# A sparse-attention and gated-MLP kernel on one core: the first batch in query thirds over all heads, with the gated MLP dealt out matmul by matmul

## The chip, the core and the metric

The kernel runs on one core of a Trainium2 chip. The core has five engines with instruction queues of their own: TensorE (PE in the profile, its weight loads PEld) multiplies matrices into the PSUM memory, VectorE (DVE) and ScalarE (ACT) work elementwise on PSUM and SBUF, GpSimd (POOL) works on SBUF, and SyncE (SP) issues most DMA transfers. Each engine takes its instructions in order. The metric is the device time of one execution in microseconds, lower is better.

## What is computed

Two stages follow each other. The first is block-sparse attention over 4 batches, 8 heads, 768 positions and head size 64. Positions form 24 blocks of 32. A block may attend to itself and its two neighbours, to the first and last block, from the first and last block, and to three sampled blocks. The mask depends on the sampled blocks and is the same for all batches and heads.

```python
scores = scale * np.matmul(q, k.transpose(0, 1, 3, 2))
scores = np.where(mask, scores, -1000000000.0)
attn = np.exp(scores - np.max(scores, axis=-1, keepdims=True))
attn = attn / (np.sum(attn, axis=-1, keepdims=True) + 1e-09)
attn_out = np.matmul(attn, v)
```

The second is a gated MLP (gMLP) per batch, on the heads side by side, x = [768, 512]:

```python
h = np.maximum(x @ w_in, 0.0)                       # 512 -> 1024
u, v = h[..., :512], h[..., 512:]
v_n = (v - mean(v)) / np.sqrt(var(v) + 1e-06)
v_s = np.einsum('ts,bsd->btd', w_spatial, v_n) + b_spatial[None, :, None]
out = (u * v_s) @ w_out
```

Each gMLP batch needs the attention of all eight heads; position t of v_s needs v_n of all 768 positions of that batch.

## The kernel before, in words

Rows 0 to 63 of the tiles `qt` and `kt` hold a head's transposed queries and keys. Rows 64 to 87 hold the mask: on the key side a one-hot row per block (`ind`), on the query side, per key block, 0 or a large negative number (`bm` times `ind`). One product over 88 rows so gives masked scores, and no maximum is subtracted.

**Attention slots.** Work goes in slots. A slot of `qk_exp` (lines 239 to 251) makes one chunk of 128 keys against all 768 queries of a head: two score matmuls of 384 columns (L244) into one of two two-bank PSUM buffers (`sc`), and one exp of 768 columns by ACT (L248) into `a_all`. A head has six slots, a batch 48, the whole kernel 192. Seven slots later (`LAG = 7`) `av` makes one chunk of 128 queries times the values: six matmuls of 65 columns (L260), the 65th column being the sum of the exps. After a head's six, `norm` (L273, L274) divides on DVE, and after a pair of heads `xtr` transposes the result, by DMA from the SP queue (L287), for the last pair of a batch by PE (L283).

**Loads.** Each pair of heads is loaded as fp32 from the SP queue (L95), cast to bf16 by POOL (L109 keys and queries, L112 values) and transposed: pairs 0 to 4 by PE (L191 one head at a time, L199 by pair) with DVE copies out of PSUM (L183, L202), later pairs by two DMA transposes (L227), keys and queries apart, and DVE copies `split_pair` (L233). The weights come by three DMAs on the POOL queue that cast on the way (L439, L446, L449). The spatial weights are transposed by PE and copied by DVE in pairs 2 and 3 (L296, L300).

**gMLP.** `moe_units` makes 24 units per batch: six v units (L332, relu and statistics on DVE, std and power on POOL at L345 and L347), six u units (L355, relu on ACT at L358, normalise on DVE at L359), six spatial units (L377, gate on DVE at L380, gated rows transposed by a DMA each, L384), six output units (L395, copies by ACT and DVE in turn, L400 and L402, store by SP, L403). A unit is four matmuls of 512 columns, a spatial unit six. When a batch's attention is complete, eight slots into the next batch, its units are queued and spread over 48 slots by a budget; a unit's matmuls always stand together. The last batch's gMLP has no attention beside it; it turns through the free PSUM buffers (`moe_ps`), evicts v on ACT (L336), and transposes its gated rows by PE (`g_tr`, L368).

**The order.** The schedule is written out by hand (`manual_schedule`): the loop over pairs and slots at the end of the kernel issues, per slot, the scores, set-up pieces, gMLP units, AV matmuls and transposes in this order, and so sets the order in every engine's queue. Before the first slot eight matmuls on zeros are issued to PE (L145).

Of the kernel before, what the change touches and what calls it, by code (L numbers as in the profile page):

```python
# [10 lines left out]
FP32 = mybir.dt.float32  # L11
# [15 lines left out]
def kernel(  # L27
# [31 lines left out]
    MASK_NEG = -300.0  # L59
    VA = D + 1  # L60
    KR = D + NB

# [9 lines left out]
    ws_nat = const.tile([128, NCH, S], BF16)  # L72
    w_spt = const.tile([128, NCH, S], BF16)
    b_col = const.tile([128, NCH], FP32)
    mhalf = const.tile([128, NCH], FP32)

    qt = [const.tile([KR, S], BF16, name=f"qt{s}") for s in range(4)]
    kt = [const.tile([KR, S], BF16, name=f"kt{s}") for s in range(4)]
    vv = [const.tile([128, 2, NCH, VA], BF16, name=f"vv{s}") for s in range(3)]
# [4 lines left out]
    def dram(src, b, h0, nh):  # L84
        return src[b, h0:h0 + nh].rearrange("h (p c) d -> p h (c d)", c=NCH)

    def st_tile(p, nm):
        st[nm, p] = work.tile([128, 2, NCH * D], FP32, tag=f"st_{nm}", bufs=2, name=f"st_{nm}")
        return st[nm, p]

    def load(p, names="qkv", eng=nc.sync):
        b, g = divmod(p, NG)
        for nm, src in (("q", q), ("k", k), ("v", v)):
            if nm in names:
                eng.dma_start(out=st_tile(p, nm), in_=dram(src, b, 2 * g, 2))  # L95
# [3 lines left out]
    def nat_tile(p, nm):  # L99
        nat[nm, p] = work.tile([128, NCH, 2, D], BF16, tag=f"nat_{nm}", bufs=2,  # L100
                               name=f"nat_{nm}")

    def cast_qk(p, nm, hs, eng):
        src = st[nm, p][:, hs].rearrange("p h (c d) -> p h c d", d=D)
        dst = nat[nm, p].rearrange("p c h d -> p h c d")[:, hs]
        if eng is nc.scalar:
            nc.scalar.activation(out=dst, in_=src, func=AF.Copy)
        else:
            eng.tensor_copy(out=dst, in_=src)  # L109

    def cast_v(p):
        nc.gpsimd.tensor_copy(  # L112
            out=vv[p % 3][:, :, :, 0:D],
            in_=st.pop(("v", p)).rearrange("p h (c d) -> p h c d", d=D))

    def prepare(p):
        for nm in "kq":
            nat_tile(p, nm)
            cast_qk(p, nm, slice(0, 2), nc.gpsimd)
        cast_v(p)  # L120

    samp_i = const.tile([NB, 2 * NR], I32)
    stq, stk = st_tile(0, "q"), st_tile(0, "k")
    nc.scalar.dma_start(out=stk[:, 0:1], in_=dram(k, 0, 0, 1))
    nc.scalar.dma_start(out=stk[:, 1:2], in_=dram(k, 0, 1, 1))
    nc.sync.dma_start(out=samp_i, in_=_listify(sampled_blocks).bitcast(I32))
    for h in range(2):
        nc.sync.dma_start(out=stq[:, h:h + 1], in_=dram(q, 0, h, 1))
    load(0, "v", nc.sync)
    load(1, "qkv", nc.sync)  # L130
    nc.sync.dma_start(out=b_col, in_=moe_b_spatial.rearrange("(p c) -> p c", c=NCH))

    ind_nat = const.tile([NB, S], BF16)
    ind = const.tile([NB, S], BF16)
    allowed = const.tile([NB, NB], FP32)
    tiny = const.tile([128, 1], FP32)
    nc.vector.memset(warm, 0.0)
    nc.vector.memset(allowed, 0.0)
    nc.vector.memset(ind_nat, 0.0)
    nc.vector.memset(tiny, 0.0)  # L140
    nc.scalar.activation(out=tiny, in_=tiny, func=AF.Exp)

    wps = psum.tile([128, 512], FP32, tag="moe", bufs=2)
    for _ in range(8):
        nc.tensor.matmul(out=wps, lhsT=warm[:, 0:128], rhs=warm, start=True, stop=True)  # L145


    colidx = const.tile([NB, NB], FP32)
    nc.gpsimd.iota(colidx, pattern=[[1, NB]], base=0, channel_multiplier=0,
                   allow_small_or_imprecise_dtypes=True)  # L150
    for c in (-1, 0, 1):
        nc.gpsimd.affine_select(out=allowed, in_=allowed, compare_op=ALU.not_equal,
                                fill=1.0, base=c, pattern=[[1, NB]], channel_multiplier=-1)
    for c in (0, NB - 1):
        nc.gpsimd.affine_select(out=allowed, in_=allowed, compare_op=ALU.not_equal,
                                fill=1.0, base=-c, pattern=[[0, NB]], channel_multiplier=1)
    nc.gpsimd.affine_select(out=ind_nat, in_=ind_nat, compare_op=ALU.not_equal, fill=1.0,
                            base=0, pattern=[[-1, NB], [0, BLK]], channel_multiplier=1)
    make_identity(nc, ident)
    nc.gpsimd.tensor_copy(out=ind, in_=ind_nat.rearrange("b (p c) -> b c p", c=NCH))  # L160

    for s in range(3):
        nc.gpsimd.memset(vv[s][:, :, :, D:VA], 1.0)
    nc.gpsimd.memset(mhalf, -0.5)

    nc.vector.memset(allowed[:, 0:1], 1.0)
    nc.vector.memset(allowed[:, NB - 1:NB], 1.0)
    nat_tile(0, "q"), nat_tile(0, "k")
    samp_f = const.tile([NB, 2 * NR], FP32)
    nc.vector.tensor_copy(out=samp_f, in_=samp_i)  # L170
    for r in range(NR):
        nc.vector.scalar_tensor_tensor(out=allowed, in0=colidx,
                                       scalar=samp_f[:, 2 * r:2 * r + 1], in1=allowed,
                                       op0=ALU.is_equal, op1=ALU.max)
    bm = const.tile([NB, NB], BF16)
    nc.vector.tensor_scalar(out=bm, in0=allowed, scalar1=1.0, scalar2=-MASK_NEG,
                            op0=ALU.subtract, op1=ALU.mult)
    cast_qk(0, "q", slice(0, 1), nc.vector)
    cast_qk(0, "k", slice(0, 1), nc.scalar)
    nc.vector.tensor_copy(out=kt[0][D:KR, :], in_=ind)  # L180

# [6 lines left out]
    def tr_head(h, nm, copy):  # L188
        ps = psum.tile([128, S], BF16, tag="moe", bufs=2)
        for c in range(NCH):  # L190
            nc.tensor.transpose(out=ps[0:D, c * 128:(c + 1) * 128], in_=nat[nm, 0][:, c, h],  # L191
                                identity=ident)
        copy((qt if nm == "q" else kt)[h][0:D, :], ps[0:D, :])

    def tr_pair(p, nm):
        src = nat.pop((nm, p))
        ps = psum.tile([128, S], BF16, tag="moe", bufs=2)
        for c in range(NCH):
            nc.tensor.transpose(out=ps[:, c * 128:(c + 1) * 128],  # L199
                                in_=src[:, c].rearrange("p h d -> p (h d)"), identity=ident)  # L200
        for h in range(2):
            nc.vector.tensor_copy(out=(qt if nm == "q" else kt)[(2 * p + h) % 4][0:D, :],  # L202
                                  in_=ps[h * D:(h + 1) * D, :])

    tr_head(0, "k", dve_copy)
    mq = psum.tile([128, 1024], FP32, tag="sc", bufs=2, name="mq")
    for hf in range(2):
        nc.tensor.matmul(out=mq[0:NB, hf * 512:hf * 512 + HALF], lhsT=bm,
                         rhs=ind[:, hf * HALF:(hf + 1) * HALF], start=True, stop=True)
# [43 lines left out]
    def av(j, qc):  # L253
# [10 lines left out]
        if qc == NCH - 1:  # L264
            a_ref.pop(j)
# [240 lines left out]
```

## Time and profile before

| what | value |
|---|---|
| median of 3 runs | 231.86 us (231.13 to 235.44) |
| profiled execution: span, first to last instruction | 228.9 us |
| mean granted TensorE clock | 0.975 |
| PE / PEld busy | 217.0 us (95%) / 130.9 us (57%) |
| ACT busy | 171.3 us (75%), of it exps 144.2 |
| DVE / POOL busy | 131.9 us (58%) / 52.8 us (23%) |
| first exp starts / 12th ends / 48th ends | 7.64 / 20.4 / 47.0 us |
| last batch's gMLP | 199.9 to 225.3 us |
| HBM read / written | 24.38 MB / 6.29 MB |

The profile is one execution; its span lies 2.96 us below the median of the runs, which hold the time around the first and last instruction as well. A busy engine in the row PE need not be a PE at its peak, since matmuls overlap and their ends are modelled: what a matmul costs in a dense row of them is the distance between the starts of two groups. In the rows by stage, the seventh number is the granted clock (1.00 is full speed), then the share of the DMA engines that was busy and the GB/s they moved. An engine that is idle costs nothing unless the chain of work runs through it.

### The profile page before, as it was taken

The page shows a single profiled execution, that of the slowest core. Times are in us where ns is not written, and L with a number is a line of the kernel's source. Part 1 is how long each engine was busy: PE and PEld are TensorE (multiplying, and loading weights), DVE is VectorE, ACT ScalarE, POOL GpSimd, SP SyncE. Part 2 cuts the span into 40 slices and gives each one's busy share as a digit, 9 for nine tenths or more (in the row PEclk, how much of TensorE's full clock was granted, in tenths as well). Part 3 has the DMA queues.
Part 4 walks back from the last instruction along what each step waited for, and adds up shares of the span by engine and source line. Part 5 has one row for each costly group of instructions (what it writes and reads, how often), then busy time and mean ns, then how long its engine had stood idle before and what let it go on. Part 6 is the DMA issues. An engine that isn't in the chain of part 4 may idle for free.

```text
span 228.9 us, 5246 instructions
## 1 busy us (share of the span) xinstructions
PE 217.0 (95%) x2105; PEld 130.9 (57%) x2134; DVE 131.9 (58%) x285; ACT 171.3 (75%) x244; POOL 52.8 (23%) x83
## 2 busy tenths in 40 slices
PE   7799999999999999999999999999999999999993
PEld 3356677766566555665656555566656555544551
DVE  6643545647996545349995344269992423575532
ACT  3668999998799767786799666977798677256341
POOL 7440560421153401210172201210250000012000
PEclk9758999999999999999999999999999999999998
DMA  6589999999418273989838364999050423520015
GB/s 212 201 244 223 356 171 217 271 249 302 149 34 219 86 143 52 275 288 288 243 70 243 64 112 82 265 327 258 3 103 3 80 49 78 198 83 0 0 47 229
DMA packets 54940, 37.31 MB, mean 163 GB/s; under 512 B 38404, under 2 KB 51204, under 8 KB 54788
## 3 DMA queue, kind: packets, MB, share of 16 engines
q1 hardware_dynamic: 53428, 33.83, 54.7%
q0 software_dynamic: 1200, 2.75, 7.1%
q10 hardware_dynamic: 288, 0.39, 0.5%
q8 instruction: 16, 0.26, 0.5%
q14 instruction: 8, 0.07, 0.2%
HBM read 24.38 MB, written 6.29 MB: 134 GB/s over the span
## 4 chain that ended last, share of the span: by engine, by line
PE 76%; ACT 17%; DVE 2%; issue 2%; DMA 1%; ACTq 0%
PE ps L244 22%; ACT a_all L248 17%; PE ps_av L260 11%; PE ps_moe L377 10%; PE ps_moe L332 7%; PE ps_moe L395 7%; PE ps_moe L355 7%; PE ps_t L377 2%; PE ps_t L332 2%; PE ps_t L395 2%; PE ps_t L355 1%; PE ps_sc L377 1%; DMA samp_i<-in_sampled_blocks_dram 1%; PE ps_sc L355 1%; PE ps_sc L395 1%
## 5 line engine op out<-in xcount | busy, mean ns | idle before, releaser
L248 ACT ACTIVATE a_all<-ps 128x768 bf16<-128x768 f32 x192 | 144.2, 810 | 32.6 <-PE ps L244 32.0
L244 PE MATMUL ps<-qt,kt 88*128 88x384 bf16 x384 | 96.0, 332 | 5.2 <-ACT a_all L248 4.1
L260 PEld LDWEIGHTS <-a_all 128*128 128x128 bf16 x1152 | 62.0, 99 | 31.8 <-issue 0.7
L260 PE MATMUL ps_av<-vv,a_all 128*128 128x65 bf16 x1152 | 68.4, 195 | 0.0
L244 PEld LDWEIGHTS <-kt 88*128 88x128 bf16 x384 | 28.4, 99 | 11.0 <-issue 7.4
L380 DVE SCALAR_TENSOR_TENSOR gn<-ps_moe,b_col,un 128x512 bf16<-128x512 f32 x18 | 13.5, 751 | 27.6 <-PE ps_moe L377 27.6
L112 POOL CAST vv<-st_v 128x768 bf16<-128x768 f32 x16 | 13.6, 850 | 52.7 <-PE ps_av L260 43.1
L377 PE MATMUL ps_moe<-vn,w_spt 128*128 128x512 bf16 x99 | 24.8, 378 | 0.5
L377 PEld LDWEIGHTS <-w_spt 128*128 128x128 bf16 x144 | 13.8, 97 | 14.3
L345 POOL TENSOR_SCALAR std<-mv 128x3 f32<-128x3 f32 x8 | 1.9, 243 | 74.0 <-DVE mv L342 61.8
L109 POOL CAST nat_k<-st_k 128x768 bf16<-128x768 f32 x15 | 12.5, 836 | 27.3 <-issue 11.5
L274 DVE TENSOR_TENSOR xn<-ps_av,rc 128x384 bf16<-128x384 f32 x32 | 17.8, 557 | 1.4 <-DVE rc L273 0.3
L332 PE MATMUL ps_moe<-w_in_t,xt 128*128 128x512 bf16 x66 | 18.1, 378 | 0.3
L395 PE MATMUL ps_moe<-w_out_t,gt 128*128 128x512 bf16 x66 | 18.1, 378 | 0.3
L355 PE MATMUL ps_moe<-w_in_t,xt 128*128 128x512 bf16 x66 | 17.7, 378 | 0.3
L341 DVE BATCH_NORM_STATS2 stats<-vsb 128x6 f32<-128x512 bf16 x24 | 16.7, 694 | 1.9 <-ACT vsb L336 1.3
L332 PEld LDWEIGHTS <-xt 128*128 128x128 bf16 x96 | 9.3, 97 | 10.0 <-issue 0.7
L402 DVE COPY osb<-ps_moe 128x512 f32<-128x512 f32 x9 | 6.2, 692 | 15.0 <-PE ps_moe L395 14.9
L355 PEld LDWEIGHTS <-xt 128*128 128x128 bf16 x96 | 9.3, 97 | 9.5
L273 DVE RECIPROCAL rc<-ps_av 128x6 f32<-128x6 f32 x32 | 6.0, 186 | 13.4 <-PE ps_av L260 13.3
L395 PEld LDWEIGHTS <-gt 128*128 128x128 bf16 x96 | 8.9, 97 | 8.4
L359 DVE TENSOR_SCALAR vn<-vsb,mv,rstd 128x512 bf16<-128x512 bf16 x24 | 12.7, 564 | 0.6 <-POOL rstd L347 0.5
(85 smaller groups left out, 181.4 us busy)
## 6 DMA issues: line engine op xcount, KB each, us to landing
st_v<-in_v_dram SPq DMA_DIRECT2D x16, 384.0 KB, 6.2
out_dram<-osb SPq DMA_DIRECT2D x24, 256.0 KB, 2.3
st_q<-in_q_dram SPq DMA_DIRECT2D x15, 384.0 KB, 4.1
st_k<-in_k_dram SPq DMA_DIRECT2D x15, 384.0 KB, 4.7
ws_nat<-in_moe_w_spatial_dram POOLq DMA_DIRECT2D x1, 1152.0 KB, 12.5
w_in_t<-in_moe_w_in_dram POOLq DMA_DIRECT2D x1, 1024.0 KB, 11.8
w_out_t<-in_moe_w_out_dram POOLq DMA_DIRECT2D x1, 512.0 KB, 12.0
st_k<-in_k_dram ACTq DMA_DIRECT2D x2, 192.0 KB, 2.9
```

Source lines behind the costliest of these rows:

```text
L112: nc.gpsimd.tensor_copy(out=vv[p % 3][:, :, :, 0:D], in_=st.pop(("v", p)).rearrange("p h (c d) -> p h c d", d=D))
L244: nc.tensor.matmul(out=ps[:, hf * 512:hf * 512 + HALF], lhsT=kt[j % 4][:, ci * 128:(ci + 1) * 128], rhs=qt[j % 4][:, hf * HALF:(hf + 1) * ...
L248: nc.scalar.activation(out=a_ref[j][:, ci, :].rearrange("p (b c) -> p b c", b=2), in_=ps.rearrange("p (b c) -> p b c", b=2)[:, :, 0:HALF], ...
L260: nc.tensor.matmul(out=av_ref[j][:, qc, :], lhsT=a_ref[j][:, ci, qc * 128:(qc + 1) * 128], rhs=vv[p % 3][:, h, ci, :], start=(ci == 0), st ...
L274: nc.vector.tensor_tensor(out=xn_ref[p][:, :, h, :], in0=ps[:, :, 0:D], in1=rc.to_broadcast([128, NCH, D]), op=ALU.mult)
L332: nc.tensor.matmul(out=ps, lhsT=xt(g)[:, tcc * 128:(tcc + 1) * 128], rhs=w_in_t[:, g, DH:DFF], start=(g == 0), stop=(g == NDM - 1))
L341: nc.vector.bn_stats(out=stats, in_=vsb[:, tcc, :])
L355: nc.tensor.matmul(out=ps, lhsT=xt(g)[:, tcc * 128:(tcc + 1) * 128], rhs=w_in_t[:, g, 0:DH], start=(g == 0), stop=(g == NDM - 1))
L359: nc.vector.tensor_scalar(out=vn[:, tcc, :], in0=vsb[:, tcc, :], scalar1=mv[:, tcc, 0:1], scalar2=rstd[:, tcc:tcc + 1], op0=ALU.subtract, ...
L377: nc.tensor.matmul(out=ps, lhsT=w_spt[:, sc, tcc * 128:(tcc + 1) * 128], rhs=vn[:, sc, :], start=(sc == 0), stop=(sc == NCH - 1))
L380: nc.vector.scalar_tensor_tensor(out=gn[:, tcc, :], in0=ps, scalar=b_col[:, tcc:tcc + 1], in1=un[:, tcc, :], op0=ALU.add, op1=ALU.mult)
L395: nc.tensor.matmul(out=ps, lhsT=gt[:, tcc, dhc, :], rhs=w_out_t[:, dhc, :], start=(dhc == 0), stop=(dhc == NDH - 1))
```

## The change

**First batch in thirds.** Batch 0 is no longer done head after head. Its 36 slots go over three thirds of the queries (256 each), within a third over the four pairs of heads, three slots a pair. A slot makes four score matmuls of 256 columns and one exp of 1024 columns; three slots later `av_third` makes eight AV matmuls; after three of these the pair's third is normalised, and transposed by PE into the unused end of the AV bank (`xtr_third`), with a DVE copy. Batches 1 to 3 keep the slots of before.

```diff
+    NT = 3
+    S0 = NT * NG * 3
+    def qk_third(u, e):
+        t, p = divmod(u, NG)
...
+        ps = psum.tile([128, 1024], FP32, tag="sc", bufs=2)
+        for i in range(4):
+            h, ci = divmod(4 * e + i, NCH)
+            nc.tensor.matmul(out=ps[:, i * TW:(i + 1) * TW],
+                             lhsT=kq[:, 2 * p + h, ci * 128:(ci + 1) * 128],
+                             rhs=kq[:, 2 * p + h, qcols(t)], start=True, stop=True)
+        out = a_ref[u].rearrange("p h c n -> p (h c n)")[:, 4 * e * TW:4 * (e + 1) * TW]
+        nc.scalar.activation(out=out, in_=ps, func=AF.Exp, scale=0.125)
+    def av_third(u, e):
...
+        for i in range(8 * e, 8 * e + 8):
+            g, ci = divmod(i, NCH)
+            h, qc = divmod(g, TC)
+            nc.tensor.matmul(out=av_ref[u][:, qc * 2 + h, :],
+                             lhsT=a_ref[u][:, h, ci, qc * 128:(qc + 1) * 128],
+                             rhs=vv[p % NVV][:, h, ci, :],
+                             start=(ci == 0), stop=(ci == NCH - 1))
+    def xtr_third(u):
+        t, p = divmod(u, NG)
+        xtr_pe(p, xn_ref.pop(u), t * TC, TC, x_ref.pop(u))
```

**Keys and queries in one tile.** `kq` holds keys and queries of eight heads, 88 rows by 2 x 768 columns a head; `vv` has six buffers for three. For batch 0 all keys and the first query third are loaded, cast and transposed first (`tr_first`, a PE group of eight per pair, two DVE copies of 64x1024), then the other two thirds (`tr_rest`). The mask rows are copied to the heads by DVE and, for heads 4 to 7, by one DMA (`block_rows`). The mask is built from iotas and comparisons on DVE, and the sampled blocks are read as integers.

```diff
-    qt = [const.tile([KR, S], BF16, name=f"qt{s}") for s in range(4)]
-    kt = [const.tile([KR, S], BF16, name=f"kt{s}") for s in range(4)]
-    vv = [const.tile([128, 2, NCH, VA], BF16, name=f"vv{s}") for s in range(3)]
+    kq = const.tile([KR, H, 2 * S], BF16, name="kq")
+    NVV = 6
...
+    ts(lim[MR], hot[MR], 1.0 - BLK, ALU.max, BLK - 1.0, ALU.min)
+    tt_op(kq[MR, 0, K_].rearrange("b (c p) -> b c p", c=NCH), hot[MR], lim[MR], ALU.is_equal)
...
+    def second_head():
+        dve_copy(kq[0:D, 1, qcols(0)], psq[D:128, 0:TW])
+        ps = k_head(1)
+        dve_copy(kq[MR, 1, 0:S + TW], kq[MR, 0, 0:S + TW])
+        dve_copy(kq[0:D, 1, K_], ps[0:D, 0:S])
+        filler(2, wps)
...
+    def tr_first(p):
+        src = nat.pop(p)
+        ps = bank()
+        for c in range(NCH + TC):
+            tr(ps, c, pair_of(src, c))
+        for h in range(2):
+            dve_copy(kq[0:D, 2 * p + h, 0:S + TW], ps[h * D:(h + 1) * D, :])
```

The eight matmuls on zeros become six, two before the first scores and two in `second_head`.

**Merged DMA transposes.** From pair 4 on, one DMA transpose takes keys and queries of a pair together, and each head is copied out by one DVE copy of 64x1536 (`split`). Gated rows are transposed two chunks at a time. The spatial weights go by DMA transposes too.

```diff
-        nc.sync.dma_start_transpose(out=tt[nm, p],
-                                    in_=nat.pop((nm, p)).rearrange("p c h d -> p (c h d)"))
+    def tr_dma(p):
+        tt[p] = work.tile([128, 2 * NCH, 128], BF16, tag="tt", bufs=2, name="tt")
+        nc.sync.dma_start_transpose(out=tt[p], in_=nat.pop(p).rearrange("p c h d -> p (c h d)"))
```

**Weights.** The three casting DMAs of the POOL queue are gone. SP loads w_in in eight pieces, w_out in four and w_spatial in six, as fp32, the first two into the four buffers of `osb`; POOL casts them.

**gMLP by single matmuls.** Every product becomes a list of single matmuls, the last of which runs the eviction. `run_queue` takes so many of them per slot that the list lasts for the slots given. Batch 0 is dealt in three parts as its thirds end, batches 1 and 2 over 48 slots each as before. v is normalised in place, the gate is written over u, and the tiles `un`, `vn`, `gt` have one buffer for two. u products stand between v products, with two u products behind the last v (in the last batch three, u3 to u5), where six stood before. The last batch transposes its gated rows by DMA, the last two chunks singly, and its last output product is made in two halves.

```diff
+        when(17, c(moe_begin, 0), lambda: deal(moe[0].in_steps(0, TC, TC), 12))
+        when(29, lambda: deal(moe[0].in_steps(TC, TC, TC), 12))
+        when(41, lambda: deal(moe[0].in_steps(2 * TC, TC, TC) + moe[0].rest_steps(), S0 + 8 + 48 - 41))
...
+    def run_queue():
+        if not queue or pace["slots"] <= 0:
+            return
+        pace["credit"] += (len(queue) - pace["credit"]) / pace["slots"]
+        pace["slots"] -= 1
+        n = int(pace["credit"] + 0.5)
+        for _ in range(min(n, len(queue))):
+            queue.popleft()()
+            pace["credit"] -= 1
...
+            if self.last:
+                seq = [(nm[0], int(nm[1])) for nm in "v0 v1 u0 v2 u1 v3 v4 u2 v5 u3 u4 u5".split()]
```

**Schedule.** The set-up pieces hang on slot numbers (`when`). For a pair p of batches 1 to 3 whose first slot is g, the loads are issued at slot g-34 (not before 14), the casts at g-21, the DMA transpose at g-18, the two `split` copies at g-5 and g-3:

```diff
+    when(0, second_head,
+         c(cast, 1, "k", PL), c(cast, 1, "qa", PL), c(cast, 0, "v", PL),
+         c(cast, 2, "k", PL), c(cast, 2, "qa", PL), c(cast, 1, "v", PL),
+         c(block_rows, slice(2, 4), slice(0, S + TW), DV))
...
+    when(10, *[c(w_in_cast, 0, g, PL) for g in range(NDM)])
+    when(10, *[c(w_in_load, 1, g) for g in range(NDM)])
+    when(14, *[c(w_in_cast, 1, g, PL) for g in range(NDM)])
...
+        when(max(14, g - 34), c(load, p, "k"), c(load, p, "q"), c(load, p, "v"))
+        when(g - 21, c(cast, p, "k", PL), c(cast, p, "q", PL), c(cast, p, "v", PL))
+        when(g - 18, c(tr_dma, p))
+        when(g - 5, c(split, p, 0))
+        when(g - 3, c(split, p, 1))
```

## The prediction

> **What bounds the kernel now.** I read the slices first, then the chain that ended last, the costliest groups, the busy time by stage, and the TensorE timeline inside one stage.
>
> ```profile
> PE   7799999999999999999999999999999999999993
> ...
> ACT  3668999998799767786799666977798677256341
> ...
> PEclk9758999999999999999999999999999999999998
> DMA  6589999999418273989838364999050423520015
> ...
> PE 76%; ACT 17%; DVE 2%; issue 2%; DMA 1%; ACTq 0%
> ...
> L248 ACT ACTIVATE a_all<-ps 128x768 bf16<-128x768 f32 x192 | 144.2, 810 | 32.6 <-PE ps L244 32.0
> ```
>
> PE is "busy" nearly throughout, but matmuls overlap in that row, so the split by stage is needed. Columns: length, then busy time of PE, PEld, DVE, ACT, POOL, granted clock, DMA share, GB/s. My cuts: first exp, 12th, 48th, start of each gMLP batch, last matmul.
>
> ```profile
> 7.64:20.40 12.76, 11.75 (x84) 6.76 (x83) 5.66 (x14) 9.32 (x13) 5.45 (x7) 0.60 0.75 203
> 20.40:47.03 26.63, 25.63 (x361) 19.39 (x361) 14.12 (x30) 26.32 (x37) 9.44 (x12) 1.00 1.11 259
> ...
> 102.82:152.90 50.08, 48.85 (x493) 29.63 (x499) 30.66 (x67) 40.15 (x57) 11.99 (x16) 1.00 0.72 186
> 152.90:199.94 47.04, 45.79 (x465) 27.53 (x471) 28.37 (x61) 33.70 (x48) 4.75 (x7) 1.00 0.40 102
> 199.94:225.27 25.33, 24.93 (x134) 11.84 (x133) 13.80 (x29) 12.43 (x21) 2.30 (x4) 1.00 0.15 56
> ```
>
> From 20.4 to 47.0 ACT is 99% busy, and on to 52.8: exps bound. From 52.8 on PE bounds (ACT 80% busy), and after 200 PE runs alone. Real matmul prices are distances between starts:
>
> ```profile
> 83.88 1.46 PE L377 MATMUL ps_moe<-vn,w_spt 128*128 128x512 bf16 x6
> 85.17 0.35 PE L260 MATMUL ps_av<-vv,a_all 128*128 128x65 bf16 x6
> 85.36 0.49 PE L244 MATMUL ps<-qt,kt 88*128 88x384 bf16 x2
> 85.69 0.35 PE L260 MATMUL ps_av<-vv,a_all 128*128 128x65 bf16 x6
> ```
>
> Six AV matmuls take 85.36-85.17 = 0.19 us (0.032 each), two score matmuls 0.33, six gMLP matmuls 85.17-83.88 = 1.29 (0.215 each). An attention slot (two scores, six AVs, one exp) is 0.52 on PE. Against that, one exp follows another every 0.74 (20 in 14.83 us on the ACT timeline). So each of 44 ACT-bound slots leaves PE 0.2 us free, some 9 us in all. A PE-bound batch needs 48x0.52 + 108x0.215 + 0.35 of transposes = 48.6 and takes 50.1.
>
> **The change, part by part.** The sum goes against the profiled span, 228.9; the median of the runs is 231.86, so I add 2.96 at the end. Every PE product stays, and so do the score columns. What moves is when gMLP of batch 0 may start: after the first query third of all heads (slot 17 of 36) instead of after the whole batch (slot 56).
>
> A, to the first exp: 6.9 (before 7.64). The mask still ends in three 0.53 us steps on DVE. The 0.68 integer cast goes; two 24x768 passes come (0.35, the nearest copy, up to 0.99, POOL's select of that shape) behind a POOL iota. Mask at about 5.1, then product, 256-column copy, four score matmuls. Ends 6.2 and 8.0.
>
> B1, slots 0 to 8, the columns of the first 12 exps: 13.3 (before 12.76). ACT's floor is 9x0.948: a 1024-column exp costs 0.74 plus 0.208, which is what the rows' 810 ns for 768 columns lie above the 602 ns of ACT's relu of 512 (L358). PE at half clock needs 36 scores at 0.213, 48 AVs at 0.065 (six slots of eight), 32 transposes at 0.14 (second head 6, three pairs 24, first xT 2; six took 0.85 there), fillers 1.7, together 16.9. DVE must deliver keys of all eight heads: six 64x1024 copies (0.55 for 768, so 0.73), mask rows for heads 1 to 3 (0.35 per 768 columns), the rest small, about 9 to 10 us in 13. Before's row is nearest; I add 0.5 for the denser copies. Ends 8.5 and 16.9.
>
> Here two rules bear. In the trace PE was 4.8 us busy of 5 between 10 and 15 us and yet the granted clock was 0.50, until 19. The Trainium skill (TensorE: Matmul & The Clock Gate, Part 1) says that one sustained busy window of about 3.4 us lifts the throttle; by that rule the clock would be full from about 6 us, B1 about 10.5 and the total 2.8 lower. The second speaks against the change, and the row stands first:
>
> ```profile
> L109 DVE CAST nat_k<-st_k 128x384 bf16<-128x384 f32 x1 | 0.9, 868 | 0.0
> ...
> L109 DVE CAST nat_q<-st_q 128x384 bf16<-128x384 f32 x1 | 0.3, 344 | 0.0
> ```
>
> The same cast took 868 ns while POOL cast and 344 with POOL idle. The skill (GPSIMD Engine Reference, Key points) says that POOL shares its SBUF interfaces with VectorE and contends with its two-port modes. POOL casts without a break from 6.5 to 13 us in the changed kernel; by the rule its SBUF-to-SBUF mask-row copies (0.45 and 0.93) cost 1.5x1.4 = 2.1 us more. The sum does not use either.
>
> B2, slots 9 to 16: 8x0.948 = 7.6; PE needs 0.73 a slot. At half clock 8x1.45 = 11.6.
>
> B3, slots 17 to 35, with 25 gMLP matmuls dealt in: ACT 19x0.948 + 2 relus at 0.60 = 19.2; PE 19x0.73 + 25x0.215 = 19.3. Both near full, so 3% as in the PE-bound batch: 19.8. Slot 36 begins at 47.6, where before ended its 48th exp at 47.0, but with 25 of 108 products done. Upper end 24.4, if the 5.4 us are not hidden at all.
>
> C, slots 36 to 91, the other 83 products: PE 56x0.52 + 83x0.215 + 0.35 = 47.3, ACT 56x0.74 + 7 evictions at 0.60 = 45.6; with 3%, 48.7. Before's same attention slots (47.03 to 102.82) took 55.8: this is the gain, 7.1. Ends 47.3 and 51.
>
> D, slots 92 to 139: PE need 48.6; before 50.08. Six-matmul lumps starved ACT and then PE (0.35 us per spatial unit); single matmuls remove about half of the 1.5: 49.3. Ends 48.6 and 50.1. A new wait stands against it: only two u products now follow the last v, 8 matmuls over 3.6 us, and the way relu, statistics, POOL's std and power (0.24 + 0.89), normalise takes about 4. DVE waits for POOL in order, with the AV normalise queued behind it.
>
> E, slots 140 on: 46.2 (before 47.04), PE need 45.8.
>
> F, the last gMLP: 108x0.215 = 23.3; the 24 gate transposes (1.4) go to DMA, hidden under four output products (3.4) as a gate transfer landed in 2.5. The wait for the last xT copy stays, 0.4. Last v to S now has three u products (2.6) plus three spatial matmuls (0.65) against relu 0.87, statistics 0.87, POOL 1.4, normalise 0.35: about 0.7 of new wait. 24.4 (before 25.33); ends 23.7 and 25.3. G: half-width last eviction, 3.3 (before 3.63).
>
> At nothing: w_spatial's 36 transposes leave PE from a stage where ACT covered them. Weights go by SP queue and POOL casts (18 casts at 0.56 to 0.84, about 12 us more on a POOL 23% busy). SP holds second-half w_in loads until POOL has cast the first half, with the loads of pairs 4 and 5 behind them; merged transposes are issued 13 slots before their split copies, where a single one landed in 3.5, worst 13. Batch 0's xT leaves the DMA queue for PE (24x0.058) and DVE.
>
> Sum: 6.9+13.3+7.6+19.8+48.7+49.3+46.2+24.4+3.3 = 219.5; with 2.96, 222.5.
>
> **Rivals.** R1, nothing hides in the exp-bound stage: with two score buffers each inserted matmul delays the next exp. For it: PE's waits of 0.35 after each spatial unit. Against: there PE ran six matmuls in a row, here one or two. Price 5.4: 227.9, within 2%.
>
> R2, slower: loads arrive late. POOL's queue puts the casts of pair 4 ahead of the std that VectorE waits for at slot 26 (37 us), and VectorE holds everything behind it. Bytes up to pair 4's v: 1536+512+1024+1536 KB of batch 0, 2048 of w_in, 1152, so 8.0 MB. At the rows' 203 GB/s to 20.4 us and 259 after, they land at 35.3, and cast, std and power end at 37.4: just in time. For it: POOL waited 8.1 and 7.4 us for loads between 20 and 47 us in before. Against: no DMA transposes run then. Each us late costs a us. Below 195 GB/s after 20.4 us it is within 2% of before, below 133 it is over 14 us late and slower than 236.5.
>
> R3, the half clock lasts: to slot 17 it costs 4 (226.5). Dense half-clock work ended it at 19 us in before; if it lasted past slot 27 the change would be slower too.
>
> **How the numbers follow.** Forecast 0.70; R1 0.11; R2 0.10, half within 2%, half slower; R3 0.09, of that 0.06 still faster, 0.03 slower. Within 2% of before (227.2 to 236.5) is about what a measurement of this kernel tells from no change. Faster 0.70+0.06 = 0.76, same 0.11+0.05 = 0.16, slower 0.08. The forecast alone spans 216 to 227 (B1 -4.8, D and F -1.4; B1 +3.6 and half of C's +2.3). The range 215 to 230 takes in R1, R3's mild form and the start of R2, and leaves out about 0.13.
>
> **What would show it.** Right: the 36th 1024-column exp ends near 47 us, PE matmuls of the w_in line before 40 us, 91 to 97 us at the start of gMLP 1, no PE row of g transposes. Wrong: ACT idle above 3 us between 28 and 47 (R1), VectorE waiting for POOL or POOL for loads near 37 us (R2), granted clock 0.5 after 21 us (R3).

## The result, and the profile after

The changed kernel takes 224.99 us (median of four runs, 223.58 to 226.25), beside 233.35 us for the kernel before on the same chip: a ratio of 0.971 with an interval of 0.964 to 0.978. The ratio takes fast executions alone, and two of the four of the kernel before (234.83 and 235.44 us) were slow ones, so it is not the quotient of the two medians. The forecast was 222.5 us and the range 215 to 230. The profiled execution took 225.78 us with a span of 224.0, so 1.8 us lie around the span, not the 2.96 that the forecast added from the kernel before.

From the page of the changed kernel: the slices, the chain's shares by engine, and the groups of the 768-column exp and of the new 1024-column exp.

```profile
PE   7939999995999999999999999999999999999993
...
ACT  4735999996799999997999887988899878256021
...
PEclk9985999999699999999999999999999999999999
DMA  6998079999999999999365779697050234620257
...
PE 67%; DMA 16%; POOL 5%; DVE 4%; SPq 3%; issue 2%; ACT 2%; POOLq 0%; DVEq 0%; ACTq 0%
...
L323 ACT ACTIVATE a_all<-ps 128x768 bf16<-128x768 f32 x144 | 114.0, 813 | 15.7 <-PE ps L319 8.2
...
L311 ACT ACTIVATE a_all<-ps 128x1024 bf16<-128x1024 f32 x36 | 35.1, 1035 | 7.8 <-PE ps L307 7.6
```

The PE row has two dents, at the third and the tenth slice (each slice is 5.6 us), and the clock row has a dent behind each, 5 and 6 tenths. The chain says what they may be: DMA had 1% of it before and has 16% now, POOL has 5%.

The stages of the changed kernel, cut at the stages of the prediction: first exp, end of the 9th and of the 36th exp of 1024 columns, the starts of the later gMLP batches, the last matmul. Columns as before (length; busy time of PE, PEld, DVE, ACT, POOL; granted clock; DMA share; GB/s).

```profile
6.74:21.99 15.25, 11.18 (x119) 8.82 (x119) 7.27 (x14) 8.88 (x9) 8.19 (x12) 0.78 1.03 297
21.99:49.60 27.61, 27.09 (x388) 22.23 (x390) 19.55 (x51) 26.91 (x30) 15.17 (x20) 1.00 0.78 236
49.60:101.27 51.67, 48.51 (x512) 30.10 (x520) 25.20 (x52) 46.27 (x65) 23.70 (x27) 0.97 1.10 265
101.27:150.00 48.73, 48.25 (x492) 29.44 (x498) 31.07 (x58) 42.06 (x58) 12.43 (x16) 1.00 0.75 184
150.00:195.90 45.90, 45.15 (x462) 27.23 (x469) 27.17 (x56) 35.69 (x49) 4.62 (x7) 1.00 0.39 88
195.90:220.04 24.14, 23.70 (x110) 10.78 (x111) 13.27 (x27) 8.79 (x15) 2.29 (x4) 1.00 0.30 82
```

| stage | before | forecast | after |
|---|---|---|---|
| A, to the first exp | 7.64 | 6.9 | 6.74 |
| B1, slots 0 to 8 | 12.86 | 13.3 | 15.25 |
| B2 and B3, slots 9 to 35 | 26.47 | 27.4 | 27.61 |
| C, slots 36 to 91 | 56.45 | 48.7 | 51.67 |
| D, slots 92 to 139 | 50.08 | 49.3 | 48.73 |
| E | 46.93 | 46.2 | 45.90 |
| F, last gMLP | 24.81 | 24.4 | 24.19 |
| G, to the end | 3.65 | 3.3 | 3.88 |

In the table, F ends with the end of the last matmul (225.23 us before, 220.09 after; the last row above stops 0.05 us short of it). The column before is cut at the same events as the column after: the first matmul of a gMLP batch starts at 103.41, 153.49 and 200.42 us, 0.5 to 0.6 us behind the cuts in the prediction, so its 55.8 us for C before are 56.45 here.

B1 and C are late, by 2.0 and 3.0 us; all other stages lie within 0.6 us of the forecast. Those two are where the dents are.

Of the signs that the prediction named, the matmuls of the w_in line came at 29.7 us (before 40), and no PE row of gate transposes is left. Three did not come as named: the 36th exp of 1024 columns ended at 49.6 us and not near 47, the second batch's gMLP began at 101.27 us and not at 91 to 97, and the clock was at half after 21 us, until 22.2 and again from 56.3, which was the sign given for R3.

**The first dent.** The chain of the changed kernel in time (start, length, what) from the first exp on:

```profile
6.74 0.26 ACT a_all L311
7.00 9.12 DMA kq<-kq
16.13 0.14 issue
16.26 1.01 PE ps L307 x4
```

One DMA is the whole chain for nine microseconds. It copies the mask rows to heads 4 to 7 (L257, 192 KB, SP's queue); the scores of the third pair of heads wait for it. What the wait does to the clock shows in short windows of the same kernel:

```profile
12.50:15.00 2.50, 0.03 (x1) 0.00 (x0) 1.76 (x4) 0.52 (x1) 0.92 (x3) 1.00 1.10 169
15.00:15.40 0.40, 0.00 (x0) 0.00 (x0) 0.00 (x0) 0.00 (x0) 0.35 (x1) 0.95 1.06 165
...
20.00:22.00 2.00, 2.00 (x17) 1.49 (x16) 1.90 (x5) 1.02 (x1) 0.00 (x0) 0.50 0.64 227
22.00:24.00 2.00, 2.00 (x38) 1.88 (x36) 1.91 (x5) 1.68 (x2) 0.44 (x1) 0.95 0.05 18
...
56.00:56.40 0.40, 0.40 (x4) 0.21 (x3) 0.40 (x3) 0.40 (x1) 0.06 (x1) 0.90 0.96 371
56.40:59.60 3.20, 3.20 (x16) 1.50 (x15) 0.59 (x2) 2.47 (x4) 3.20 (x2) 0.50 1.12 266
59.60:60.00 0.40, 0.40 (x9) 0.28 (x8) 0.40 (x1) 0.01 (x1) 0.40 (x2) 0.84 1.07 399
```

PE has nothing to do from 12.5 us; in the second row the clock falls to half (0.95 over 0.4 us puts the fall at 15.36), and it stays there until 22.2 (0.95 over the 2 us from 22), though PE is busy without a break from 16.3 on. So the wait is paid twice: once as a wait, once as slow matmuls behind it. The last three rows belong to the second dent.

**The second dent.** POOL's timeline of the changed kernel (start, busy time, instruction; in brackets the idle time before it and its releaser), then VectorE's and TensorE's:

```profile
50.19 3.07 POOL L401 CAST ws_b<-ws_f 128x768 bf16<-128x768 f32 x2 [3.27 <-DMA ws_f<-in_moe_w_spatial_dram]
53.35 0.23 POOL L459 TENSOR_SCALAR std<-mv 128x2 f32<-128x2 f32 x1
```

```profile
49.69 0.18 DVE L456 BATCH_NORM_AGGREGATE mv<-stats 128x2 f32<-128x6 f32 x1
...
54.42 0.41 DVE L178 TENSOR_SCALAR vn<-vn,mv,rstd 128x512 bf16<-128x512 bf16 x1 [3.34 <-POOL rstd L461]
...
54.95 0.42 DVE L335 TENSOR_TENSOR xn<-ps_av,rc 128x256 bf16<-128x256 f32 x1
```

```profile
55.44 0.28 PE L213 MATMUL ps_av<-ident,xn 128*128 128x128 bf16 x2 [2.50 <-DVE xn L335]
```

The variance was there at 49.9, but POOL's queue held two casts of the spatial weights ahead of std, and these first waited 3.27 us for their load and then took 1.55 us each (1.68 is the mean of all six). VectorE waited in order, the AV normalise stood behind the v normalise, and PE stood 2.5 us for it. ACT idled 2.17 us, and from 56.3 to 59.7 us the clock was at half.

### The profile page after: what moved, and what is told of

The parts are those of the page before. It is cut to its first block, busy times and chain, and to the rows that moved or that the text cites. A ratio compares the mean times of both kernels' runs of the same rounds, so it can differ in the third digit from the quotient of the medians.

```text
span 224.0 us, 5207 instructions
## 1 busy us (share of the span) xinstructions
PE 209.0 (93%) x2095; PEld 130.7 (58%) x2128; DVE 128.5 (57%) x276; ACT 172.0 (77%) x228; POOL 69.5 (31%) x104
## 4 chain that ended last, share of the span: by engine, by line
PE 67%; DMA 16%; POOL 5%; DVE 4%; SPq 3%; issue 2%; ACT 2%; POOLq 0%; DVEq 0%; ACTq 0%
PE ps_moe L427 26%; PE ps L319 21%; PE ps_av L359 12%; DMA kq<-kq 4%; DMA ws_f<-in_moe_w_spatial_dram 4%; DMA st_v<-in_v_dram 3%; DMA out_dram<-osb 3%; PE ps_t L427 3%; PE ps L307 2%; POOL ws_b L401 2%; SPq L491 2%; DMA st_qa<-in_q_dram 2%; DVE stats L455 1%; POOL rstd L461 1%; PE ps_sc L427 1%
## 5 line engine op out<-in xcount | busy, mean ns | idle before, releaser
L323 ACT ACTIVATE a_all<-ps 128x768 bf16<-128x768 f32 x144 | 114.0, 813 | 15.7 <-PE ps L319 8.2
L319 PE MATMUL ps<-kq 88*128 88x384 bf16 x288 | 71.4, 329 | 0.5 <-ACT a_all L323 0.2
L359 PEld LDWEIGHTS <-a_all 128*128 128x128 bf16 x864 | 46.7, 98 | 20.3 <-issue 0.5
L319 PEld LDWEIGHTS <-kq 88*128 88x128 bf16 x288 | 28.3, 98 | 31.6 <-issue 1.6
L311 ACT ACTIVATE a_all<-ps 128x1024 bf16<-128x1024 f32 x36 | 35.1, 1035 | 7.8 <-PE ps L307 7.6
L307 PE MATMUL ps<-kq 88*128 88x256 bf16 x144 | 23.4, 287 | 4.4 <-DMA kq<-kq 3.7
L481 DVE SCALAR_TENSOR_TENSOR un<-ps_moe,b_col,un 128x512 bf16<-128x512 f32 x18 | 13.5, 748 | 15.6 <-PE ps_moe L427 13.2
L178 DVE TENSOR_SCALAR vn<-vn,mv,rstd 128x512 bf16<-128x512 bf16 x24 | 13.1, 570 | 12.9 <-POOL rstd L461 12.9
L307 PEld LDWEIGHTS <-kq 88*128 88x128 bf16 x144 | 13.9, 101 | 10.0 <-issue 4.7
L335 DVE TENSOR_TENSOR xn<-ps_av,rc 128x384 bf16<-128x384 f32 (+1 forms) x36 | 18.4, 512 | 1.2
L455 DVE BATCH_NORM_STATS2 stats<-vn 128x6 f32<-128x512 bf16 x24 | 16.6, 692 | 2.7 <-ACT vn L451 2.1
```

The costliest lines, as they stand in the source:

```text
L178: nc.vector.tensor_scalar(out=out, in0=in0, scalar1=s1, scalar2=s2, op0=o0, **kw)
L307: nc.tensor.matmul(out=ps[:, i * TW:(i + 1) * TW], lhsT=kq[:, 2 * p + h, ci * 128:(ci + 1) * 128], rhs=kq[:, 2 * p + h, qcols(t)], start=T ...
L311: nc.scalar.activation(out=out, in_=ps, func=AF.Exp, scale=0.125)
L319: nc.tensor.matmul(out=ps[:, hf * 512:hf * 512 + HALF], lhsT=kq[:, j % H, ci * 128:(ci + 1) * 128], rhs=kq[:, j % H, S + hf * HALF:S + (hf ...
L323: nc.scalar.activation(out=a_ref["h", j][:, ci, :].rearrange("p (b c) -> p b c", b=2), in_=ps.rearrange("p (b c) -> p b c", b=2)[:, :, 0:H ...
L335: nc.vector.tensor_tensor(out=out, in0=ps[:, :, 0:D], in1=rc[:, 0:n].to_broadcast([128, n, D]), op=ALU.mult)
```

## The experiments

e1 to e4 are each one edit of the changed kernel, x1 joins two of them, and x2 to x4 are edits of x1; all compute everything. Spans and stages are of the profiled execution, the rest are medians with the ratio to the kernel before of the same call. The four executions of the changed kernel have spans of 221.8 to 224.5 us, so a difference of a microsecond or two between two spans shows nothing by itself; the stages have to show where it lies.

**e1, the mask rows on another queue.** Theory: SP's queue makes the DMA late. Rival: it is late wherever it is issued.

```diff
-    block_rows(slice(4, H), slice(0, S + TW), nc.sync)
+    block_rows(slice(4, H), slice(0, S + TW), nc.scalar)
```

> The DMA that copies the mask rows to heads 4 to 7 is issued from ACT's queue and no longer from SP's; nothing else changes. Theory (it lands 9.1 us after its issue because the loads already in SP's queue stand ahead of it): it lands within about 3 us, as the 192 KB key loads of ACT's queue do, PE waits less than 0.5 us for it, the ninth 1024-column exp ends near 16.5 us where it ended at 21.98, and the span is some 4 us shorter, near 220. Rival (the copy from SBUF to SBUF of 24 rows is slow by itself, whatever its queue): it lands after 7 us or more, PE waits 2 us or more, and the span stays within 1 us of 224.

223.32 us (0.9661, 0.962 to 0.970); span 221.7. ACT's timeline of this kernel, and PE's:

```profile
7.06 1.41 ACTq L257 DMA_DIRECT2D kq<-kq  x1
8.51 5.71 ACT L311 ACTIVATE a_all<-ps 128x1024 bf16<-128x1024 f32 x6 [2.74 <-PE ps L307]
```

```profile
15.29 0.60 PE L307 MATMUL ps<-kq 88*128 88x256 bf16 x4 [1.57 <-DMA kq<-kq]
```

The DMA still took from 7.06 to 15.2 us, 8.1 us on an otherwise empty queue, and its issue held the first exp back to 8.51. So the order on SP is not what makes it slow. The loads keep the DMA engines full in that time (a share of 1.03 over B1 in the changed kernel, 1.07 from 13 to 15 us in e1), and the trace has the DMA's packets begin 4.1 and 4.5 us after the issue. That they wait behind the loads' packets fits, but no run here took the loads away, and none excludes that a copy of this form is slow by itself, which was the rival. Why it is slow stays open. Because the first exps ran later and the DMA landed a microsecond earlier, PE stood for it only 1.57 us, and the 9th exp ended at 19.59 instead of 21.99. The clock still fell, at 17.0.

**e2, the mask rows by VectorE.**

```diff
-    block_rows(slice(4, H), slice(0, S + TW), nc.sync)
...
+    when(2, c(block_rows, slice(4, 6), slice(0, S + TW), DV))
+    when(5, c(block_rows, slice(6, H), slice(0, S + TW), DV))
```

> No DMA for the mask rows of heads 4 to 7: VectorE copies them, in two copies of 24x2048 (0.68 us for such a copy in the changed kernel). Theory (that wait and the half clock behind it are the 5 to 6 us that the first nine slots lie above their exps): the ninth exp ends near 16.5 us, the granted clock stays 1.00 from 9 to 22 us, the span falls by 4 to 6 us, to 218 to 220. Rival (VectorE, which then has 1.4 us more to do in the first six slots, or POOL waiting for loads, is late next): the ninth exp ends after 18.5 us, or the gain is given back before slot 36, and the span falls by under 2 us.

221.84 us (0.9585, 0.954 to 0.963); span 220.9. The 9th exp ends at 16.87, 5.1 us earlier, so B1 is 10.6 us and not 15.25. By the 36th exp 3.4 us of it are left, and the span falls by 3.1, less than the 4 to 6 expected: VectorE, with the copies added, is then what comes late (between 9 and 50 us score products waited 1.5 us for its copies, their weight loads 2.2). The copies also cost more than the same shape in the changed kernel. VectorE's timeline of the changed kernel, then of e2 (a third, at 10.59 us, took 1.12):

```profile
7.78 0.68 DVE L259 COPY kq<-kq 24x2048 bf16<-24x2048 bf16 x1
```

```profile
7.32 1.19 DVE L259 COPY kq<-kq 24x2048 bf16<-24x2048 bf16 x1
...
14.46 1.21 DVE L259 COPY kq<-kq 24x2048 bf16<-24x2048 bf16 x1
```

In e2 POOL casts nearly without a break while these copies run. In the changed kernel it is POOL that paid: its cast beside the 0.68 us copy took 1.17 us, where the same cast with VectorE idle (at 10.51 us) took 0.83. This is the rule of the Trainium skill that the prediction set beside the sum (GPSIMD Engine Reference, Key points: POOL shares its SBUF interfaces with VectorE), and the rows agree with it: a third to a half of a microsecond a copy.

**e3, zeros in the wait, to keep the clock up.** Eighteen matmuls on zeros stand where PE waits for the mask rows.

```diff
-    when(5, c(mask_rows, 1, 2, dve_copy))
+    when(5, c(mask_rows, 1, 2, dve_copy), c(filler, 18, wps))
```

> The wait for the mask rows stays, but 18 matmuls on zeros (3.9 us at full clock) are put on PE in front of the score matmuls that wait. Theory (the idle PE lets the clock fall, and the half clock from 15.5 to 22 us costs time of its own): the granted clock stays 1.00 from 15 to 22 us, the exps of slots 6 to 8 follow each other every 0.95 us, the ninth ends near 20.4 us where it ended at 21.98, and the span falls by 1.5 us. Rival (after the wait the slots are held by VectorE's key copies, not by the clock): the ninth exp ends between 21.5 and 22.5 us at full clock and the span stays within 0.5 us.

223.70 us (0.971, 0.965 to 0.977); span 222.2. PE's timeline of this kernel, then ACT's:

```profile
7.90 1.03 PE L171 MATMUL wps<-warm 128*128 128x512 bf16 x2
...
14.63 3.83 PE L171 MATMUL wps<-warm 128*128 128x512 bf16 x17 [0.16 <-issue]
18.30 0.60 PE L307 MATMUL ps<-kq 88*128 88x256 bf16 x4
```

```profile
18.94 3.89 ACT L311 ACTIVATE a_all<-ps 128x1024 bf16<-128x1024 f32 x4 [3.97 <-PE ps L307]
```

Behind the wait the 7th to 9th exps take 2.97 us (18.94 to 21.91) instead of 4.68 (17.31 to 21.99): the half clock is worth 1.7 us. No time came of it, though. The ninth exp ends at 21.91, as in the changed kernel, where 20.4 was expected, and the 36th at 51.18, 1.6 us later. There are two reasons. The last of the mask rows landed at 16.23, but PE was on the zeros until 18.47, so the zeros made the end of the wait. And this execution started slowly. The trace holds no record of the clock before its first change, and the views count that time as 1.00, but the matmuls tell: the two on zeros at 7.90 take 1.03 us, where the same two take 0.60 in the changed kernel (at 7.09). Here the clock rose only at 10.47 us, there at 5.12; from then on it is 1.00 to the last matmul.

The lower span comes from elsewhere: the second dent is almost gone here (C 48.48 us), without any edit at it. It thus hangs on when the slots of the loads, casts and std fall, a matter of a microsecond or two.

**e4, the spatial weights' casts behind std.** Casts of the spatial weights' last four pieces, loads of the last two and two of the three DMA transposes move to later slots; nothing else does.

```diff
-        when(23 + 2 * i, c(ws_load, i))
-        when(27 + 2 * i, c(ws_cast, i))
+    for i, at_load, at_cast in ((0, 23, 27), (1, 25, 29), (2, 27, 37), (3, 29, 38),
+                                (4, 39, 48), (5, 40, 49)):
...
```

> The POOL casts of the spatial weights 2 to 5 stand behind the std and power of the second and third part of batch 0, not ahead of them (casts at slots 37, 38, 48, 49, their loads and DMA transposes moved behind accordingly). Theory (VectorE waits 3.3 us at 51 to 54 us for a std that stands in POOL's queue behind casts which wait for loads, the AV normalise and so PE wait behind VectorE, and the clock falls): no wait of VectorE for the power of POOL above 1 us between 45 and 62 us, no PE gap of 2.5 us at 53 us, granted clock 1.00 from 56 to 60 us, and the stretch from the 36th exp to the start of the second batch's gMLP falls from 51.7 to about 48.5 us, the span by 3 us. Rival (that stretch is bound by PE and ACT anyway, or the later weights stop the spatial products): it stays above 50.5 us.

222.48 us (0.9645, 0.960 to 0.969); span 220.0. POOL's timeline of this kernel, to be held against that of the second dent:

```profile
49.60 0.23 POOL L459 TENSOR_SCALAR std<-mv 128x2 f32<-128x2 f32 x1 [3.06 <-DVE rc L334]
49.91 0.73 POOL L461 TENSOR_TENSOR rstd<-std,mhalf 128x2 f32<-128x2 f32 x1
50.61 3.14 POOL L401 CAST ws_b<-ws_f 128x768 bf16<-128x768 f32 x2
```

POOL now waits for VectorE and not the other way round. C is 48.12 us; 3.5 of the 51.67 were this wait and the half clock behind it.

**x1, both repairs** (e2 and e4), and six buffers instead of four for the output rows and the fp32 weights.

> Mask rows of heads 4 to 7 by VectorE, casts of the spatial weights behind the std, and six buffers in place of four for the fp32 weights and output rows. Theory (the two stalls are apart in time and add up; with four buffers the last output copies waited 0.3 to 0.6 us for stores, and the second half of w_in waited for POOL's casts): the 36th exp ends near 46 us, the second batch's gMLP starts near 94.3, span 216.5 to 217.5, some 7 us under the changed kernel and 3.5 under the copies on VectorE alone. Rival (with the first wait gone the loads are the bound, and the second stall only moves): the stretch from the 36th exp to the second batch's gMLP stays above 50 us and the span above 219.5.

217.69 us (217.26 to 219.26; 0.9426, 0.939 to 0.947); span 216.0, clock 1.00. This is the fastest kernel of the study: faster than the changed kernel and than the one before. Its stages:

```profile
6.24:16.33 10.09, 8.66 (x117) 6.71 (x118) 8.12 (x14) 8.88 (x9) 8.34 (x12) 1.00 1.05 355
16.33:44.84 28.51, 27.68 (x394) 22.23 (x393) 21.52 (x54) 27.22 (x31) 15.28 (x21) 1.00 0.95 277
44.84:93.01 48.17, 47.70 (x521) 29.50 (x520) 29.12 (x52) 46.08 (x64) 23.50 (x27) 1.00 1.09 268
93.01:141.74 48.73, 48.73 (x500) 29.45 (x499) 31.05 (x58) 42.06 (x58) 12.32 (x16) 1.00 0.76 192
```

The repairs add up: the span falls by 8.0 us, where alone they took 3.1 and 4.0 (by the medians 7.3, 3.2 and 2.5). What x1 gains beyond the sum may be the six buffers: by the 36th exp it is 1.4 us ahead of e2 (44.84 and 46.20), but no run changed the buffers alone. D is the same to the hundredth, so neither repair touches anything behind C. The remaining three kernels take one part of the change out of x1.

**x2, no gMLP product before slot 41.** The 25 early matmuls are dealt with the other 83.

```diff
-    when(17, c(moe_begin, 0), lambda: deal(moe[0].in_steps(0, TC, TC), 12))
-    when(29, lambda: deal(moe[0].in_steps(TC, TC, TC), 12))
-    when(41, lambda: deal(moe[0].in_steps(2 * TC, TC, TC) + moe[0].rest_steps(), S0 + 8 + 48 - 41))
+    when(41, c(moe_begin, 0),
+         lambda: deal(sum((moe[0].in_steps(t, TC, TC) for t in (0, TC, 2 * TC)), [])
+                      + moe[0].rest_steps(), S0 + 8 + 48 - 41))
```

> As the kernel with both repairs, but the gMLP matmuls of batch 0 (25 of them by slot 36 there) are all dealt from slot 41 on: the thirds are kept, the early start is taken away. Theory (the early matmuls were hidden behind exps): the 36th exp ends at most 1.5 us earlier than with them (two relus fewer on ACT), the stretch behind it grows by 32 matmuls at 0.215, some 6 us, and the span is 4.5 to 6 us longer than with both repairs. Rival (inserted matmuls delayed the exps one for one): the 36th exp ends 4 to 5 us earlier and the span stays within 1 us.

227.09 us (0.9785, 0.972 to 0.985); span 225.1, 9.1 more than x1. That is more than 25 matmuls can be, and VectorE's timeline says why it can't be read as their price:

```profile
58.04 0.18 DVE L455 BATCH_NORM_AGGREGATE mv<-stats 128x2 f32<-128x6 f32 x1
64.56 0.41 DVE L178 TENSOR_SCALAR vn<-vn,mv,rstd 128x512 bf16<-128x512 bf16 x1 [6.33 <-POOL rstd L460]
```

The late deal moved the second std to where POOL's queue held a cast of the spatial weights, three of a pair and four of w_out: the second dent again, at 6.3 us. The run is inconclusive on its question.

**x4, the same with POOL's queue cleared:** the last two casts of the spatial weights at slots 57 and 58, their transpose at 59, w_out's casts at 60.

> Late deal once more (no gMLP product before slot 41), with both repairs, and now the last two casts of the spatial weights (slots 57 and 58 instead of 48 and 49), their transpose and the casts of w_out (60 instead of 52) stand behind the statistics' std on POOL's queue. Theory that the stall at 62 to 67 us was the queue's and not the late deal's: the 36th exp ends at 42.5 as before, the 25 products then cost 5.4 us of PE in the PE-bound stretch, which becomes 48.2 + 5.5 = 53.7 us, and the span is 216.0 - 2.4 + 5.5 = 219.1 (218.5 to 220.5): the early deal is worth about 3 us. Rival, that the late deal itself costs 9 us (products and attention together starve ACT): the stretch stays at 58 to 59.5 us and the span at 224 to 225, with no wait of VectorE for rstd above 1 us.

221.56 us (0.9589, 0.951 to 0.967); span 220.0. The exp-bound part and the stretch behind it, to be held against the second and third row of x1:

```profile
16.58:43.17 26.59, 24.81 (x368) 20.91 (x369) 15.81 (x44) 25.28 (x28) 14.35 (x18) 1.00 0.86 267
43.17:96.94 53.77, 52.61 (x537) 32.30 (x547) 34.12 (x62) 48.13 (x67) 24.28 (x29) 1.00 1.02 242
```

C is 53.77 us (53.7 was expected), 5.6 longer than in x1; the exp-bound part is 1.9 shorter. Two ACT relus of 0.60 are in those 1.9, so of 5.4 us of early matmuls about 0.7 are not hidden. The span differs by 4.0. The first exp came 0.8 us later here (7.03 and 6.25), which is not the edit's doing: in this execution the clock rose at 6.66 us, in x1 at 4.71, and the two matmuls on zeros ahead of the first scores take 1.03 us and not 0.60. By the ninth exp 0.2 of it are left (16.58 and 16.34). The early deal is worth 5.6 - 1.9 = 3.7 us.

**x3, products in lumps again.** `run_queue` pops a product's matmuls together once half its credit is there.

```diff
-        n = int(pace["credit"] + 0.5)
-        for _ in range(min(n, len(queue))):
-            queue.popleft()()
-            pace["credit"] -= 1
+        while queue:
+            n = 1
+            while n < len(queue) and not getattr(queue[n], "first", False):
+                n += 1
+            if pace["credit"] < n / 2:
+                break
+            for _ in range(n):
+                queue.popleft()()
+            pace["credit"] -= n
```

> As the kernel with both repairs, but a product's four or six gMLP matmuls are taken from the list together, at the same mean rate. Theory (in lumps PE starves ACT and then waits for it, 0.35 us per spatial product): the stretches of the second and third batch's gMLP (48.7 and 45.5 us in the changed kernel) are 1 to 1.5 us longer each, the batch-0 part some 1 us, the span 3 to 4 us longer than with both repairs. Rival (those stretches became shorter for other reasons, such as fewer transposes and copies): within 0.7 us of the span with both repairs.

227.72 us (0.984, 0.981 to 0.987); span 225.7, 9.7 more than x1. D and E are 50.34 and 47.42, what they were in the kernel before (50.08 and 46.93) and 1.6 and 1.5 more than in x1, about as expected. The surprise is C: 54.11, 5.9 more than x1, so that the span grew by 9.7 and not by the 3 to 4 expected. Stage C and D of this kernel, then the timelines of PE and of ACT around one lump in C:

```profile
45.64:99.75 54.11, 50.16 (x522) 30.91 (x521) 26.91 (x49) 44.96 (x65) 22.56 (x26) 1.00 0.89 234
99.75:150.09 50.34, 49.53 (x501) 29.68 (x499) 30.34 (x59) 40.83 (x58) 12.28 (x16) 1.00 0.72 185
```

```profile
77.17 1.46 PE L426 MATMUL ps_moe<-vn,w_spt 128*128 128x512 bf16 x6
78.47 0.49 PE L318 MATMUL ps<-kq 88*128 88x384 bf16 x2
...
79.85 0.48 PE L318 MATMUL ps<-kq 88*128 88x384 bf16 x2 [0.18 <-ACT a_all L322]
...
81.07 1.46 PE L426 MATMUL ps_moe<-vn,w_spt 128*128 128x512 bf16 x6
```

```profile
78.99 2.96 ACT L322 ACTIVATE a_all<-ps 128x768 bf16<-128x768 f32 x4 [0.98 <-PE ps L318]
```

From lump to lump are 3.90 us (81.07-77.17) for four slots of 0.52 and one lump of 1.29, together 3.37: half a microsecond is lost at each. During the lump ACT runs out of scores and idles for 0.98 us; afterwards PE waits for the exps that are late. C has 18 lumps, six of them of six matmuls, and 5.9 us over 18 is 0.33 each. D has 24 lumps and loses 1.6; ACT is 86% busy there (42.06 of 48.73 in x1) and can catch up, in C it is 96% busy (46.08 of 48.17) and cannot. That ACT's slack makes the difference is read from these rows; no run changed it alone.

## Why the prediction was right, and where it was not

The sign, the size and the bounds held: 224.0 us of span against 219.5 summed. Part of this is luck: the two late stages cost 4.9 us, and 1.2 of these were covered by a wrong term around the span and 1.1 by D, E and F. Step by step:

- **A, B2 and B3, D, E and F held**, each within 0.6 us. For A the closeness is luck: the first exp starts at 6.25 us in x1, where the clock rose at 4.71, at 6.74 in the changed kernel (5.12) and at 7.22 in e3 (10.47), with the same work ahead of it. 25 gMLP matmuls do fit beside the exps (x4), so the price of R1 did not arise. That D loses its lumps' stalls was right in mechanism and too small in size: the forecast took half of the 1.5, all of it came.
- **B1 failed, 13.3 against 15.25.** The step is "the rest small": the DMA of the mask rows to heads 4 to 7 was in effect costed at nothing, with no row that bounded it. It took 9.12 us. Without it (e2, x1) B1 is 10.6 and 10.1, less than forecast, because the clock is then full from 4.5 and 4.7 us on: the forecast had added to a row of the kernel before in which the mean granted clock was 0.60. So two errors stood against each other. R3's mechanism came behind a wait (1.7 us by e3), and not from the thin start that the prediction feared.
- **C failed, 48.7 against 51.67.** The step is the entry "Weights go by SP queue and POOL casts" under what was put at nothing, with the casts at 0.56 to 0.84 us each. Those of the spatial weights read with a stride and take 1.55 to 1.91, and they stand ahead of std. This is R2's mechanism, POOL in order behind a load, at another load (spatial weights, not pair 4) and at a price of 3.5 us instead of the 14 that would have decided the sign. With it removed C is 48.12 (e4) and 48.17 (x1), as summed.
- **The reason given for C was half of it.** The prediction put all of C's gain down to the early start of gMLP and counted single matmuls in D alone. The early start with lumps (x3) leaves C at 54.11, single matmuls with the late start (x4) at 53.77, both together give 48.17, and the kernel before had 56.45. Each by itself is worth 2 to 3 us in C, both 8.3, if the kernel before may stand for the one with neither; it differs in more, and no run of the new kernel has lumps with the late deal. That ACT has no slack left to repair what a lump does once the early deal has made the stage short is read from the rows and not shown.
- **The rest of the change was not taken apart.** From x1, 12.9 us of span under the kernel before, the early deal takes 3.7 and the single matmuls 9.7. What the merged transposes, the weights by SP and POOL, and the spatial and gate transposes off PE are worth no run shows.
- **G was 3.88, not 3.3.** The store alone, from the end of the last copy to the end of the span, is 3.2 us (220.76 to 223.97). Ahead of it VectorE's last copy waited 1.26 us for an earlier store, since `osb` has four buffers:

```profile
220.34 0.42 DVE L203 COPY osb<-ps_sc 128x256 f32<-128x256 f32 x1 [1.26 <-DMA out_dram<-osb]
```

  With six buffers (x1) no copy waits for a store, and G was still 3.85: there the store took 3.4 and one copy stood 0.5 behind the other. The forecast left too little for the store.
- **The 2.96 us around the span were 1.8.** The forecast set the median of three executions against the span of one. Execution by execution the kernel before has 1.8 as well (230.70 us with a span of 228.9, in e1's call). With 1.8 the sum would have given 221.3; the error hid part of the two misses.

## What to carry to other kernels

A DMA of 192 KB from SBUF to SBUF, issued beside a full set of loads, took 7.8 to 9.4 us in the four kernels here that have it (changed, e1, e3, e4), on either of two queues, where the loads beside it took 5.7 to 8.3 (medians by tile). If a matmul waits for such a DMA, cost it by a load's row of the same stretch and never at nothing. When work is added to an in-order engine that also carries a small step of a latency chain (POOL with its std here), find the slot at which the chain comes due and put the bulk behind it; every later edit that shifts the slots (x2) must be looked at again for this. By the rows of x3, splitting PE's side work into single matmuls pays most where the engine that it starves has least slack (0.33 us a lump with ACT 96% busy, 0.07 with 86%), so cost it stage by stage against that engine's busy share.

## What was not expected of the hardware

- A copy of 192 KB from SBUF to SBUF took 9.12 us on one queue (7.8 in e4, 9.4 in e3) and 8.1 on another, with the DMA engines filled by loads.
- The clock changes on a grid. In the changed kernel it falls at 15.36 and 56.32 us and returns at 22.18 and 59.73: the distances are 6.82, 34.14 and 3.41, which is 2, 10 and 1 times 3.41. In the kernel before, half clock lasts from 9.0 to 19.24, three times 3.41 (from 0.75 over 8 to 10 us and 0.88 over 19 to 20); in e1 from 16.97 to 20.38, once. Between two grid points PE was idle for 2.8 of 3.4 us (12.5 to 15.36), for 2.5 (52.9 to 55.4) or, in e1, for only 1.57, and the clock fell at the next point, even where PE was at work again by then. Idle time alone does not set the border: 1.23 us between 5.59 and 9.00 in the kernel before were enough, 1.41 between 14.76 and 18.17 in e2 were not. After a fall the clock came back, in every trace here, behind the first stretch between points in which PE had no gap. At the start this does not hold: in e3 the stretch from 3.65 to 7.06 had no gap, and the clock rose at 10.47. The Trainium skill (TensorE: Matmul & The Clock Gate, Part 1) states a free-running window of about 3.4 us, and the traces agree with that. It asks for an idle window before the fall, where here 1.2 to 1.6 us of idle in a window could be enough. Read as a grid, the same rule also fits the half clock of the kernel before, which the prediction had held against it: its first two windows at half clock had gaps of 0.2 us each, its third none.
- A cast of 128x768 from fp32 took POOL 0.83 us with a contiguous source and 1.55 to 1.91 with the strided one.
